# Random-feature attention and a feed-forward layer on one core: the weights' sign by a parametric ReLU, a fused sum and maximum for the keys, wider query instructions, float16 sums over the keys from unit 8 on

## The chip, the cores and the metric

The kernel runs on one core of a Trainium2 chip. The metric is the device time of one execution in microseconds, as the median of several runs; a run with the hardware profiler gives the trace. Engines are named as the profile names them: PE (TensorE, matmuls), PEld (its weight loads), DVE (VectorE), ACT (ScalarE), POOL (GpSimd), SP (SyncE, which issues the DMAs).

## The reference, cut to what matters

```python
# q, k, v: (8 batches, 8 heads, 576 tokens, 64); omega: (128, 64)
q_s, k_s = q * D ** -0.25, k * D ** -0.25
def phi(x):                               # 128 positive features
    h = x @ omega.T - (x * x).sum(-1, keepdims=True) / 2
    return np.exp(h - h.max(-1, keepdims=True)) / np.sqrt(128)
q_p, k_p = phi(q_s), phi(k_s)
kv = einsum('bhsm,bhsd->bhmd', k_p, v)    # sum over the keys
z  = k_p.sum(2)
attn = einsum('bhsm,bhmd->bhsd', q_p, kv) / (einsum('bhsm,bhm->bhs', q_p, z)[..., None] + 1e-6)
x = attn, heads side by side              # (4608 tokens, 512)
out = gelu(x @ w_in) @ w_out              # 512 -> 2048 -> 512; the weights come as float64
```

The term with the squares is the same for all features of a token and drops out with the maximum. So per pair of heads the kernel needs the projection by omega, a maximum per token, the exponential, the sum over the keys of exp(k) times (v, 1), and its product with exp(q).

## The kernel before, in words

**Attention** goes by units: one batch and two heads, 32 units of 2 x 576 tokens, four per batch. Units 0 to 7 are plain: float32 matmuls throughout. Units 8 to 31 are split: an operand becomes a high part and the rest, so that PE runs a quicker format. In a split unit `x_high` (L743, ACT) and `x_low` (L748, POOL) make the parts of q and k; `proj` (L756) projects the keys, two tiles of 128 tokens at a time into one PSUM tile, the product with omega's high part beside that with its rest; `proj_lo` (L760, ACT) copies the second half to SBUF; `proj_add` adds both halves (L769, DVE) and takes the negated maximum over the 128 features (L770, DVE). `k_shift` (L774, POOL) adds it. The queries are projected with the features on the partitions (`proj_q`, L778), turned in blocks by DVE (`q_blocks`, L781 and L783), their maxima combined and added (`q_shift`, L804). One `exps` (L555, ACT) then exponentiates keys and queries of the unit. `q_back` (L807, DVE) turns the queries back in four quarters of 288 columns, `q_high` (L810, ACT) rounds them, `q_low` (L813, DVE) takes the rest.

The sum over the keys has two forms. `kv` (L562) is a float32 matmul per tile; units 0 to 11 use it, each with its own v load (L512). Units 12 to 31 use `kv_split` (L853): exp(k) goes scaled into a float16 part (`k_high`, POOL's L307) and its rest (`k_low`, L842), v into a float16 pair by a scale of its batch (`v_a` L831, `v_b` L834; the scale comes from `v_max`, L877, and a chain of small steps), and two float16 matmuls per tile do the sum. v comes for a whole batch in one load (L524) into SBUF that block 0's weights held before. `num` (L619) multiplies by exp(q), `den` (L630, L624 for plain units) and `rcp` (L635 to L637) take the reciprocal, `div` (L667, L670) writes x.

**The feed-forward layer** goes by blocks of tokens: 256, 256, ten of 384 and 256. Block 0 is computed in float32 (`mm1` L1017, `mm2` L1043). Later blocks use float16 pairs, three matmuls per product (L1022; L1046 to L1048), with `gelu` (L1030), `g_high` (L1034) and `g_low` (L1038) between. Block 0 needs x of units 0 to 3 alone.

**The weights** come as float64, in 16 pieces (eight of w_in, eight of w_out) through two raw buffers (loads L373). Per piece `w_hi` (L377, ACT) scales the high words, read as float32, by 2^-112, which moves the exponent's bias; `w_lo` (L380, ACT) scales the low words; `w_shift` (L383, DVE) shifts the high words left by 3, which drops the sign; `w_sign` (L386, DVE) takes the sign bit of the raw word back in; `w_round` (L389, POOL) adds the low words' share; `w_max` (L392, DVE) takes the largest magnitude, from which the scales of the float16 pairs come (L419 and on).

**What sets the order.** No instruction is written at its place. A planner (`Planner`) holds all steps with a cost per step and a due time, and emits per engine the ready step that is due first; rings of buffers hold steps back. Due times come from `STARTS` (per block), `UDUE` (per half unit) and `OFF` (per step), and from bonuses in `X`. An engine then takes its instructions in exactly this order; so what waits holds what stands behind it.

## Time and profile before

| | |
|---|---|
| median of 3 runs | 990.48 us (990.17 to 991.42) |
| the profiled execution | 989.08 us, its span 986.9 us |
| granted PE clock, mean | 0.99 |
| busy: PE, DVE, ACT, POOL | 965.6, 759.7, 722.1, 338.5 us |
| moved by DMA | 70.91 MB |

In the rows below "x" is a count. A row of a stage gives each engine's busy time in the stretch, then the clock that was granted to PE. A row of a group gives the line, engine and operation, the tiles, the count, then after the bar the busy time in us and the mean ns of one, then the idle time of the engine just before them and who ended it. Float32 matmuls are two PE instructions each in the trace (a sum over the keys of one unit, nine matmuls, is x18). Matmuls overlap in the pipe, so their mean is longer than what one adds.

### The profile page before, as it was taken

The page shows a single profiled execution, that of the slowest core. Times are in us where ns is not written, and L with a number is a line of the kernel's source. Part 1 is how long each engine was busy: PE and PEld are TensorE (multiplying, and loading weights), DVE is VectorE, ACT ScalarE, POOL GpSimd, SP SyncE. Part 2 cuts the span into 40 slices and gives each one's busy share as a digit, 9 for nine tenths or more (in the row PEclk, how much of TensorE's full clock was granted, in tenths as well). Part 3 has the DMA queues.
Part 4 walks back from the last instruction along what each step waited for, and adds up shares of the span by engine and source line. Part 5 has one row for each costly group of instructions (what it writes and reads, how often), then busy time and mean ns, then how long its engine had stood idle before and what let it go on. Part 6 is the DMA issues. An engine that isn't in the chain of part 4 may idle for free.

```text
span 986.9 us, 17389 instructions
## 1 busy us (share of the span) xinstructions
PE 965.6 (98%) x5996; PEld 607.4 (62%) x5996; DVE 759.7 (77%) x1824; ACT 722.1 (73%) x1538; POOL 338.5 (34%) x528
## 2 busy tenths in 40 slices
PE   7789999999999999999999999999999999999998
PEld 6566676666666665666655666566656665555576
DVE  6988968988998989999988889888888897421111
ACT  6957849777888888888888877878778777442233
POOL 2334411345256435534443543544235431100000
PEclk8979999999999999999999999999999999999999
DMA  9854403432122131122312131112013100000000
GB/s 263 261 167 152 142 15 98 140 99 71 48 70 60 49 102 58 48 57 73 102 36 70 49 111 49 49 48 82 25 38 90 26 2 33 1 22 12 1 33 22
DMA packets 50647, 70.91 MB, mean 72 GB/s; under 512 B 18560, under 2 KB 27136, under 8 KB 50560
## 3 DMA queue, kind: packets, MB, share of 16 engines
q1 hardware_dynamic: 50560, 69.81, 23.8%
q8 instruction: 48, 0.79, 0.3%
q14 instruction: 39, 0.32, 0.1%
HBM read 60.36 MB, written 9.44 MB: 71 GB/s over the span
## 4 chain that ended last, share of the span: by engine, by line
PE 83%; DVE 8%; ACT 5%; DMA 2%; issue 1%; POOL 0%; SPq 0%; ACTq 0%; DVEq 0%
PE h L1022 32%; PE acc L1046 10%; PE acc L1048 10%; PE acc L1047 10%; PE at L619 3%; PE h L1017 3%; PE acc L1043 2%; PE at L778 2%; PE at L756 2%; PE at L853 2%; PE at L562 2%; PE at L531 1%; DVE gl L1038 1%; DMA raw<-in_w_in 1%; DVE nm L770 1%
## 5 line engine op out<-in xcount | busy, mean ns | idle before, releaser
L1022 PE MATMUL h<-xh,wih 128*128 128x384 f16 (+1 forms) x768 | 243.9, 318 | 1.2 <-DVE gl L1038 1.0
L1022 PE MATMUL h<-xh,wil 128*128 128x384 f16 (+1 forms) x768 | 243.7, 317 | 0.0
L1022 PE MATMUL h<-xl,wih 128*128 128x384 f16 (+1 forms) x768 | 243.7, 317 | 0.0
L748 POOL TENSOR_TENSOR r<-xt,r 64x256 fp32r<-64x256 f32 (+2 forms) x216 | 163.4, 775 | 187.7 <-ACT r L743 144.5
L1038 DVE SCALAR_TENSOR_TENSOR gl<-h,bs,gh 128x384 f16<-128x384 f32 (+1 forms) x192 | 113.1, 590 | 132.6 <-ACT gh L1034 131.1
L1046 PE MATMUL acc<-woh,gh 128*128 128x512 f16 (+1 forms) x544 | 205.3, 377 | 0.0
L1048 PE MATMUL acc<-wol,gh 128*128 128x512 f16 (+1 forms) x544 | 204.5, 376 | 0.0
L1047 PE MATMUL acc<-woh,gl 128*128 128x512 f16 (+1 forms) x544 | 204.5, 376 | 0.0
L1022 PEld LDWEIGHTS <-wih 128*128 128x128 f16 x1536 | 147.4, 98 | 83.0 <-issue 1.1
L1030 ACT ACTIVATE h<-h,bs 128x384 f32<-128x384 f32 (+1 forms) x192 | 102.7, 536 | 89.8 <-PE h L1022 85.8
L1034 ACT ACTIVATE gh<-h,bs 128x384 f16<-128x384 f32 (+1 forms) x192 | 107.7, 561 | 68.8 <-PE acc L1048 56.2
L1022 PEld LDWEIGHTS <-wil 128*128 128x128 f16 x768 | 75.1, 98 | 45.7 <-issue 4.0
L1048 PEld LDWEIGHTS <-gh 128*128 128x128 f16 x560 | 54.8, 98 | 62.6
L743 ACT CAST r<-xt 128x256 fp32r<-128x256 f32 (+2 forms) x216 | 81.4, 408 | 13.8 <-PE at L778 7.3
L1046 PEld LDWEIGHTS <-gh 128*128 128x128 f16 x560 | 54.6, 97 | 51.5 <-issue 1.1
L1047 PEld LDWEIGHTS <-gl 128*128 128x128 f16 x560 | 54.9, 98 | 46.1 <-issue 0.3
L670 DVE TENSOR_TENSOR w<-at,rt 64x128 f32<-64x128 f32 (+6 forms) x168 | 54.5, 325 | 3.4
L389 POOL TENSOR_TENSOR w<-w 128x1024 int32<-128x1024 int32 x12 | 29.7, 2474 | 66.0 <-DVE w L386 32.9
L756 PE MATMUL at<-om,r 128*128 128x256 f32 x216 | 50.6, 329 | 0.0
L778 PE MATMUL at<-r,om 128*128 128x288 f32 x192 | 49.3, 350 | 0.0
L813 DVE TENSOR_TENSOR ql<-qt,qh 128x288 fp32r<-128x288 f32 x96 | 43.9, 475 | 1.8 <-ACT qh L810 1.2
L630 ACT ACTIVATE dt<-at,vsc 64x288 f32<-64x288 f32 x80 | 39.7, 496 | 5.7 <-PE at L619 3.9
(223 smaller groups left out, 1773.6 us busy)
## 6 DMA issues: line engine op xcount, KB each, us to landing
xt<-in_kT SPq DMA_DIRECT2D x56, 288.0 KB, 4.0
xt<-in_qT SPq DMA_DIRECT2D x56, 288.0 KB, 3.7
out_x<-o SPq DMA_DIRECT2D x35, 256.0 KB, 2.0
raw<-in_w_in SPq DMA_DIRECT2D x16, 512.0 KB, 6.2
raw<-in_w_out SPq DMA_DIRECT2D x16, 512.0 KB, 4.4
w<-in_v SPq DMA_DIRECT2D x5, 1280.0 KB, 7.6
vt<-in_v SPq DMA_DIRECT2D x12, 320.0 KB, 3.8
out_x<-o SPq DMA_DIRECT2D x2, 128.0 KB, 1.9
```

The source lines that it names most:

```text
L670: nc.vector.tensor_tensor(x[r, c0:c1], ps[r, r0:r1], rt[r, r0:r1], op=ALU.mult)
L743: nc.scalar.copy(G['r', u, i][:, 0:b - a], xf[:, a:b])
L748: nc.gpsimd.tensor_tensor(r, xf[D:, a:b], r, op=ALU.subtract)
L756: nc.tensor.matmul(o[:, t], r[:, t * P:(t + 1) * P], om, start=True, stop=True)
L778: nc.tensor.matmul(G['pp', u, NK + g][:, 0:HS], om[:, i], G['r', u, NK + g], start=(i == 0), stop=(i == 1))
L1022: nc.tensor.matmul(h[:, 0:t], w, (G['xh', n, j], G['xh', n, j], G['xl', n, j])[k][:, 0:t], start=(i == 0), stop=(i == 3 * NJ - 1))
L1030: nc.scalar.activation(h, h, AF.Gelu, scale=G['bs', n][:, 2:3])
L1034: nc.scalar.activation(G['gh', n, c][:, 0:t], G['h', n, c][:, 0:t], AF.Copy, scale=G['bs', n][:, 3:4])
L1038: nc.vector.scalar_tensor_tensor(G['gl', n, c][:, 0:t], G['h', n, c][:, 0:t], G['bs', n][:, 3:4], G['gh', n, c][:, 0:t], op0=ALU.mult, op1 ...
L1046: nc.tensor.matmul(acc, gh[:, s], woh[:, c, c0:c1], start=(c == 0), stop=False)
L1047: nc.tensor.matmul(acc, gl[:, s], woh[:, c, c0:c1], start=False, stop=False)
L1048: nc.tensor.matmul(acc, gh[:, s], wol[:, c, c0:c1], start=False, stop=(c == NF - 1))
```

## The change

Line numbers of the changed kernel are a little higher; the steps keep their names.

- **Sign.** `w_hi` becomes a parametric ReLU with the same scale and a slope of 2^32 for negative words. That adds 32 to the exponent field of negative words alone, and `w_shift` moves just that bit into the sign's place. `w_sign` is gone, and `w_shift` is the last reader of the raw high words.
- **Maximum.** For pieces 2 and 3 of w_in, `w_abs` on ACT takes the sum of magnitudes (an upper bound of the largest) in place of `w_max` on DVE.
- **Sum and maximum of the keys.** `proj_add` is one fused instruction per tile of 128, with the maximum not negated; `k_shift` subtracts it. 216 tiles, and each is built as two instructions, one of 128x128 and one that writes 128x1; before there were 120 sums and 120 maxima, most of two tiles.
- **Queries.** `q_back`, `q_high` and `q_low` take two quarters at once: 576 columns, 48 of each instead of 96. The rings of `ql` tiles go from four of 288 to two of 576.
- **Float16 sums** from unit 8 instead of unit 12. Four v loads of a unit go, one of a batch comes.
- **Numbers of the planner**: all of `STARTS`, `UDUE`, `OFF`, some of `X` and some costs; `unit_split` is written in three parts with the same steps. So the order changes everywhere.

```diff
-X = dict(fb=94.6, fbp=-752.88, fb0=364.35, fbb=95.45, fbw=0.0, pm=0.144, tsw=1.28, wmaxp=0, plain=8, kvp=12, eb0=8, ttr=0)
+X = dict(fb=1419.17, fbp=-418.17, fb0=70.16, fbb=27.19, fbw=0.0, pm=0.15, tsw=1.28, wmaxp=0, plain=8, kvp=8, eb0=8, ttr=1,
+         pair=0, amax=12, qm=1, xm=0, km=0, prelu=1)
-STARTS = (352.72, 544.34, 271.08, 310.17, 157.51, 294.13, 523.44, 1198.62, 642.88, 445.45, 511.92, 981.52, 1405.68, 529.37)
+STARTS = (207.4, 1014.76, 655.98, -86.82, 177.65, 324.46, 422.08, 1469.57, 896.45, 1238.21, 1606.05, 2531.59, 2425.69, 1171.74)
...
     def w_hi(pc):
         hf = raw(pc)[2].bitcast(F32)
-        nc.scalar.activation(hf, hf, AF.Copy, scale=2.0 ** -112)
+        if X['prelu']:
+            nc.scalar.activation(hf, hf, AF.Prelu, scale=2.0 ** -112, alpha=2.0 ** 32)
+        else:
+            nc.scalar.activation(hf, hf, AF.Copy, scale=2.0 ** -112)
...
+    def w_abs(pc):
+        s = pc.l if pc.l is not None else raw(pc)[1]
+        nc.scalar.activation(s.bitcast(F32), pc.w, AF.Abs, accum_out=wmax[:, pc.win, pc.i:pc.i + 1])
...
-        op('DVE', 1.21, w_sign, pc, r=[rk, rk + ('hi',)], w=bk)
+        if not X['prelu']:
+            op('DVE', 1.21, w_sign, pc, r=[rk, rk + ('hi',)], w=bk)
...
-        if not X['wmaxp'] >> win & 1:
+        if X['amax'] >> (i + 8 * (1 - win)) & 1:
+            op('ACT', 1.3, w_abs, pc, r=bk, w=[('wmax', win, i)] + (pc.lk if pc.l is not None else [rk, rk + ('lo',)]))
+        elif not X['wmaxp'] >> win & 1:
             op('DVE', 1.21, w_max, pc, r=bk, w=[('wmax', win, i)])
...
+    def qv(t, g):
+        v = t.rearrange("p (a h s) -> p a h s", a=2, h=2)
+        return v[:, :, g] if X['qm'] else v[:, g // 2:g // 2 + 1, g % 2]
+
     def q_back(u, g):
-        nc.vector.transpose(G['qt', u, g], u.ef[:, slice(*XG[NK + g])])
+        nc.vector.transpose(G['qt', u, g], qv(u.ef[:, R2:], g))
     def q_high(u, g):
-        nc.scalar.copy(G['qh', u][:, g * HS:(g + 1) * HS], G['qt', u, g])
+        nc.scalar.copy(qv(G['qh', u], g), G['qt', u, g])
     def q_low(u, g):
-        nc.vector.tensor_tensor(G['ql', u, g], G['qt', u, g], G['qh', u][:, g * HS:(g + 1) * HS], op=ALU.subtract)
+        nc.vector.tensor_tensor(G['ql', u, g], G['qt', u, g], qv(G['qh', u], g), op=ALU.subtract)
...
-        for x, g in enumerate((0, 2, 1, 3)):
+        for x, g in enumerate((0, 1) if X['qm'] else (0, 2, 1, 3)):
```

The branch of `proj_add` that `ttr=1` now takes stood in the program before:

```python
for t in range(t0, t1):
    nc.vector.tensor_tensor_reduce(u.et[:, t], pp_k(u, i)[:, t - t0, 0], G['lo', u, i][:, t - t0], 1.0, -3e38, ALU.add, ALU.max, G['nm', u][:, t:t + 1])
```

Three places of the new order. The first is SP's queue at the very start; om is omega, xt are q and k of a unit, raw the weights. Before:

```order
1 L516 DMA xt<-in_kT 128x576
2 L516 DMA xt<-in_qT 128x576
3 L516 DMA xt<-in_kT 128x576
4 L516 DMA xt<-in_qT 128x576
5 L336 DMA om_66<-in_omT 64x128 x2
6 L373 DMA raw<-in_w_in 128x4x256 x4
```

And after:

```order
1 L338 DMA om_66<-in_omT 64x128 x2
2 L528 DMA xt<-in_kT 128x576
3 L528 DMA xt<-in_qT 128x576
4 L528 DMA xt<-in_kT 128x576
5 L528 DMA xt<-in_qT 128x576
6 L375 DMA raw<-in_w_in 128x4x256 x4
```

Omega's two loads moved from the fifth place to the first.

The second is DVE where x of unit 3 (xa) is written for block 0, and the last queries of unit 4 are shifted (et<-at,nm); rt and rc belong to the reciprocal, w_71 are the weights, wmax their maxima. Before:

```order
95 L386 SCALAR_TENSOR_TENSOR w_71<-raw,w_71 128x1024
96 L635 STREAM_TRANSPOSE rt<-dt 128x288
97 L636 RECIPROCAL rc<-rt 128x9
98 L637 STREAM_TRANSPOSE rt<-rc 128x288
99 L543 TENSOR_REDUCE nm<-at 128x4
100 L667 TENSOR_TENSOR xa<-acc,rt 128x256
101 L667 TENSOR_TENSOR xa<-acc,rt 128x32
102 L543 TENSOR_REDUCE nm<-at 128x4
103 L552 TENSOR_TENSOR et<-at,nm 128x512 x2
```

And after:

```order
87 L555 TENSOR_REDUCE nm<-at 128x4 x2
88 L648 STREAM_TRANSPOSE rt<-dt 128x288
89 L649 RECIPROCAL rc<-rt 128x9
90 L650 STREAM_TRANSPOSE rt<-rc 128x288
91 L564 TENSOR_TENSOR et<-at,nm 128x512
92 L680 TENSOR_TENSOR xa<-h,rt 128x256
93 L680 TENSOR_TENSOR xa<-h,rt 128x32
94 L564 TENSOR_TENSOR et<-at,nm 128x512
95 L397 TENSOR_REDUCE wmax<-w_71 128x1
```

The sign step ahead of it is gone, as six more above it are; one of the two last shifts moved ahead of xa. Above the place stand three maxima of weights now (L397), and five before (L392); two have become ACT's.

The third is PE at the sum over the keys of unit 8, between matmuls of the feed-forward layer (acc). Before, with vt the unit's v and et its exponentials:

```order
720 L1047 MATMUL acc<-woh,gl 128x512
721 L1048 LDWEIGHTS gh
722 L1048 MATMUL acc<-wol,gh 128x512
723 L562 MATMUL at<-vt_73,et 128x65 x8
724 L562 MATMUL at<-vt_73,et 128x130
725 L1046 LDWEIGHTS gh
726 L1046 MATMUL acc<-woh,gh 128x512
```

And after, with vb the float16 pair of v and w_71 the float16 exponentials:

```order
842 L1084 MATMUL acc<-wol,gh 128x512
843 L880 LDWEIGHTS w_71
844 L880 MATMUL at<-vb,w_71 128x129
845 L880 LDWEIGHTS w_71
846 L880 MATMUL at<-vb,w_71 128x65
847 L880 LDWEIGHTS w_71
848 L880 MATMUL at<-vb,w_71 128x65
849 L880 LDWEIGHTS w_71
850 L880 MATMUL at<-vb,w_71 128x129
851 L1082 LDWEIGHTS gh
852 L1082 MATMUL acc<-woh,gh 128x512
```

The sum is no longer one piece: its 18 float16 matmuls stand in groups with feed-forward matmuls between them.

## The prediction

> **What bounds the kernel now.** I read the page's busy row first, then the stages, then what TensorE (PE) waited for.

> ```profile
> span 986.9 us, 17389 instructions
> PE 965.6 (98%) x5996; PEld 607.4 (62%) x5996; DVE 759.7 (77%) x1824; ACT 722.1 (73%) x1538; POOL 338.5 (34%) x528
> ```

> The stages, each row with the stretch in us, its length, then the busy time of PE, weight loads, DVE, ACT and POOL, then the granted clock, the DMA share and GB/s:

> ```profile
> 0.00:25.00 25.00, 18.85 (x162) 16.26 (x163) 16.00 (x33) 15.72 (x45) 5.58 (x9) 0.86 0.92 264
> 25.00:50.00 25.00, 19.34 (x173) 14.20 (x174) 23.52 (x53) 22.79 (x61) 7.40 (x5) 0.97 0.85 254
> 50.00:75.00 25.00, 20.55 (x114) 15.47 (x113) 21.46 (x49) 14.60 (x23) 8.77 (x5) 0.75 0.55 166
> 75.00:100.00 25.00, 25.00 (x129) 16.08 (x126) 21.59 (x34) 18.47 (x27) 9.02 (x13) 1.00 0.43 148
> 200.00:800.00 600.00, 599.09 (x3668) 367.76 (x3666) 530.41 (x1344) 489.82 (x1078) 269.20 (x436) 1.00 0.21 62
> 900.00:987.00 87.00, 83.14 (x554) 53.96 (x552) 13.91 (x26) 28.85 (x57) 0.00 (x0) 1.00 0.05 16
> ```

> There are two regimes. From 75 us on PE is full; what shortens DVE, ACT or POOL there is worth nothing until one of them becomes late, and only PE work counts. Before 75 us PE is idle for 6.15 + 5.66 + 4.45 = 16.3 us and part of the time at a lower clock, while DVE is nearly full from 25 to 75. That is the second place where time can come from. At the end PE idles 3.9 us behind its last matmul, which the change doesn't touch. What PE waited for in the start, with the total in us, the times and the longest:

> ```profile
> PE at L600 <- ACT et L555: 3.3, 1, 3.3
> PE at L531 <- DVE om L339: 2.5, 1, 2.5
> PE at L531 <- ACT w L547: 1.8, 1, 1.8
> PE h L1017 <- DVE xa L667: 1.1, 1, 1.1
> ```

> The chain of waits behind these goes through the weights' DVE steps (start, us):

> ```profile
> 40.37 1.23 DVE w L386
> 61.45 0.43 DVE xa L667 x2
> 63.00 0.69 DVE et L552
> 63.71 2.13 ACT et L555
> ```

> L386 is the sign step that the change drops, and it stood on the chain. L667 writes the last rows of x that the first FFN block needs.

> **The PE work: float16 sums from unit 8.** The float32 sum over the keys (L562) takes 2.01 us of the chain per unit, for units 8 to 11, in a stretch where PE is full. The float16 sum (L853) has 18 matmuls per unit, so x360 are 20 units. The second row below is the chain's shares by line, the third the group (busy, mean ns of one, idle before):

> ```profile
> 195.25 2.01 PE at L562 x18
> by line: PE h L1022 32.1%; PE acc L1046 10.3%; PE acc L1048 10.2%; PE acc L1047 10.2%; PE at L619 3.1%; PE h L1017 2.8%; PE acc L1043 2.5%; PE at L778 2.4%; PE at L756 2.2%; PE at L853 1.6%; PE at L562 1.6%; issue 1.2%; PE at L531 1.1%; DVE
> L853 PE MATMUL at<-vb,w 128*128 128x65 f16 (+1 forms) x360 | 34.1, 212 | 0.0
> ```

> 1.6% of 986.9 is 15.8 us, 0.79 us per unit; four units go from 8.0 to 3.2 us: **-4.9 us**, all on the path. The busy column would give 34.1 / 20 = 1.70 us per unit and a gain of only 4 x 0.31 = 1.2 us, but a busy span holds the drain of each matmul, which lies under the next one; I keep 1.2 as the poor end.

> **The start.** In the stretch that ends when block 0 may begin, the stage row, then in it the busy time of L386 and of the maximum L392 alone, then the group of the 1024-wide ACT pass:

> ```profile
> 10.00:62.00 52.00, 42.69 (x363) 32.32 (x360) 48.08 (x99) 43.60 (x112) 16.96 (x11) 0.89 0.82 239
> 10.00:62.00 52.00, 8.51 (x7) 0.89 0.82 239
> 10.00:62.00 52.00, 6.05 (x5) 0.89 0.82 239
> L377 ACT ACTIVATE raw<-raw 128x1024 f32<-128x1024 f32 x16 | 18.6, 1164 | 0.6 <-DMA raw<-in_w_in 0.5
> ```

> DVE loses seven sign steps (8.5 us) and, by the new order, two of the five maxima (2.4 us): 48.1 becomes 37.2. ACT gains the two passes that replace those maxima, at the L377 row's 1.16 us: 43.6 becomes 45.9, and the Prelu in place of the scaled copy keeps L377's size (same tile, same count of operands but one constant; between 0 and +0.1 us each). So ACT is the next limit, and the stage can shrink by at most 52 - 45.9 = 6.1 us. ACT idles 8.4 us in it today, mostly behind DVE; I leave it 2.1 and take **-4** (ends -1 and -6.1).

> The omega load now stands first on SyncE, ahead of four loads of q and k, instead of fifth. PE waited 2.5 us for L339 behind it; the first k load is issued two DMAs later:

> ```profile
> 2.60 1.20 SPq L336 DMA_DIRECT2D om<-in_omT x2
> 0.74 0.39 SPq L516 DMA_DIRECT2D xt<-in_kT  x1
> SPq L373 <- DVE w L386: 25.8, 7, 7.9
> ```

> So 1.2 us of the 2.5 are lost again: **-1.3** (ends 0 and -2.5). The last row is SyncE's queue: loads of the next weights waited 25.8 us, in 7 waits, for L386 to release a raw buffer. The buffers come free one step earlier now; with DMA at 0.82 of its time I give that no gain of its own. The 3.3 us for the exponentials of unit 4 (L555) hang on L552 in a DVE queue that is 11 us lighter; ACT's own work ahead of them stays. I take **-2** (0 to -3.3).

> Two stretches of the start ran at a lower granted clock:

> ```profile
> 47.50:57.50 10.00, 8.64 (x55) 5.93 (x57) 8.05 (x20) 5.79 (x14) 2.55 (x2) 0.66 0.58 171
> 65.00:72.50 7.50, 6.62 (x29) 6.50 (x30) 6.10 (x14) 6.45 (x12) 2.37 (x1) 0.55 0.45 148
> ```

> Their loss is 8.64 x 0.34 = 2.9 and 6.62 x 0.45 = 3.0 us. One follows a wait of 1.8 us, the other one of 3.3. Shorter waits may spare one; I take **-3** (0 to -5.9). [...]

> **What lies beside PE, at no price while PE is full.** The groups that price it:

> ```profile
> L769 DVE TENSOR_TENSOR et<-at,lo 128x256 f32<-128x256 f32 (+1 forms) x65 | 25.2, 388 | 2.2 <-ACT lo L760 2.0
> L770 DVE TENSOR_REDUCE nm<-et 128x2 f32<-128x256 f32 (+1 forms) x65 | 25.6, 394 | 2.2
> L864 DVE TENSOR_TENSOR kvz<-at,kvs 128x128 f32<-128x128 f32 x20 | 5.7, 283 | 2.9 <-ACT kvs L860 2.7
> L894 DVE TENSOR_REDUCE vexp<-cg 32x1 f32<-32x4 f32 x13 | 1.8, 136 | 0.7 <-ACT cg L890 0.7
> L807 DVE STREAM_TRANSPOSE qt<-et 128x288 f32<-128x288 f32 x52 | 22.8, 460 | 3.6 <-ACT et L555 3.5
> L813 DVE TENSOR_TENSOR ql<-qt,qh 128x288 fp32r<-128x288 f32 x96 | 43.9, 475 | 1.8 <-ACT qh L810 1.2
> L884 DVE STREAM_TRANSPOSE ct<-cm 128x32 f32<-128x32 f32 x13 | 2.7, 205 | 0.0
> L842 DVE SCALAR_TENSOR_TENSOR w<-w 128x256 f16<-128x256 f32 (+1 forms) x50 | 21.2, 462 | 0.0
> L834 DVE SCALAR_TENSOR_TENSOR vb<-w,vsc,vb 128x640 f16<-128x640 f32 x20 | 17.9, 897 | 2.8 <-ACT vb L831 2.5
> L877 DVE TENSOR_REDUCE vmax<-w 128x1 f32<-128x640 f32 x20 | 15.8, 807 | 0.3 <-DMA w<-in_v 0.3
> ```

> The fused sum and maximum is one 128-wide instruction and one that writes 128x1, per tile. No row shows it. The nearest are L864 (two inputs, one in PSUM, 128 wide) and L894 (one column): 283 + 136 = 0.42 us. Before, a pair of tiles took 388 + 394, 0.39 us a tile. I take no change; the ends are 0.28 (the second part hidden) and 0.55 (two cycles per element by the slope below), -24 to +35 us of DVE over 216 tiles. The wider query instructions: (460 - 205) / 256 = 1.0 ns per column, so 576 columns cost 0.76 us and two of them replace four, for the transpose and the subtraction: 4 x (460 + 475) - 2 x (760 + 775) = 0.67 us per unit, 16 us over 24 units. Units 8 to 11 add L834, L877, five of L842, L864 and a 256-wide subtraction, about 4.5 us of DVE each, less about 0.5: +16 us. So DVE in 200 to 800 stays near 530 of 600 and PE covers all of it; if that cover went, each us of DVE over 600 would be a us of time. The one tight place is units 8 to 11, between 130 and 280 us, where the 16 us fall together and the wide instructions give back only 2.7; I put **+2** (0 to +6) there.

> **Sum.** The profiled execution is 989.08 us, its span 986.9 and 2.2 around it. -4.9 - 4 - 1.3 - 2 - 3 + 2 = -13.2, so 975.9. The median of the runs before, 990.48, is 1.4 above the profiled one: forecast **977.3**. All good ends give -22.7 (967.8), all poor ends +3.8, but they would have to come together.

> **Rivals.**
> *The start stays as long.* Loads and ACT set it, not DVE: DMA is at 0.82 there and ACT at 43.6 of 52, before two passes are added. Against it stand the waits for L386 and L667. Then only -4.9 and -1.3 remain: 984.
> *The start collapses.* All of it goes to ACT's floor and the clock stays up: -4.9 - 6.1 - 2.5 - 3.3 - 5.9 = -22.7: 968.
> *PE waits at the new sums, and the kernel is slower.* For units 8 to 11 the sum now needs v's maximum, its scales, both halves of v (L831, L834) and the split exponentials (POOL's L307, L842). PE takes its queue in order, so the FFN matmuls queued behind L853 wait too, and the load of v for two units' batches stands in SyncE's queue ahead of later q and k. The steps a unit gains are about 4.5 us of DVE. If PE waits more than 13.2 / 4 = 3.3 us per unit, the gain is gone; at 5 us and 20 in all it is 997. Against it: for units 12 on, PE idled 0.0 us ahead of L853.
> *The fused instruction isn't what it says.* DVE has 69.6 us idle in 200 to 800; it becomes the bound only from 0.39 + 69.6 / 216 = 0.71 us a tile on, well above the range.

> **How the numbers follow.** Forecast 0.68, the long start 0.15, the short one 0.08, PE waiting at the new sums 0.07, the slow fused instruction 0.02. The range runs from 967 (the short start) to 987 (the long start with the gain of the sums halved, and a us for the tight place) and leaves out little more than the slower cases. What a measurement here can tell from no change is about 0.2%, 2 us. Faster: 0.68 + 0.08 + most of the long start, 0.87; within 0.2%: the long start's poor end, 0.05; slower 0.08.

> **What would show it.** PE full from about 65 us instead of 75, with less than 9 us idle before; DVE under 40 us and ACT near 46 in the stretch up to block 0; the sums of units 8 to 11 at about 0.8 us of the chain each; fused tiles near 0.42 us; PE still over 99% in 200 to 800. It is wrong if PE shows waits at L853's successor in 180 to 280 us, if DVE passes 95% after 200 us, or if PE's idle time before 75 us stays near 16 us.

## The result, and the profile after

The changed kernel takes 980.18 us (median of 4 runs, 979.91 to 980.60), the kernel before 990.33 on the same chip (4 runs, 988.29 to 991.42). The ratio is 0.9901, with a 95% interval of 0.9889 to 0.9913: 10 us faster, where 13.2 were worked out.

The profiled execution took 980.60 us with a span of 978.4. The busy row of the page:

```profile
span 978.4 us, 17554 instructions
PE 960.2 (98%) x5996; PEld 598.8 (61%) x5996; DVE 716.2 (73%) x1935; ACT 729.0 (75%) x1507; POOL 355.8 (36%) x552
```

TensorE (PE) issues as many matmuls as before and is busy 5.4 us less; the span fell by 8.5, so 3.1 us come from its idle time. VectorE (DVE) lost 43.5 us of work. The stages, with the columns of before (stretch, length, busy PE, weight loads, DVE, ACT, POOL, granted clock, DMA share, GB/s):

```profile
0.00:25.00 25.00, 17.90 (x135) 14.66 (x137) 10.17 (x28) 14.37 (x38) 5.60 (x9) 0.80 0.89 251
25.00:50.00 25.00, 23.98 (x231) 18.10 (x227) 21.58 (x56) 23.86 (x67) 7.78 (x5) 1.00 0.82 252
50.00:75.00 25.00, 21.91 (x138) 16.47 (x137) 20.37 (x51) 19.50 (x31) 10.47 (x10) 0.93 0.61 179
200.00:800.00 600.00, 597.83 (x3692) 363.58 (x3691) 513.56 (x1455) 498.51 (x1042) 272.52 (x441) 1.00 0.21 59
```

PE's idle time before 75 us is 7.10 + 1.02 + 3.09 = 11.2 us, where it was 16.3. Between 200 and 800 us it is 2.2 us, where it was 0.9. The stretch up to block 0, and below it the longest rows of what PE waited for in the whole run (total us, times, longest):

```profile
10.00:62.00 52.00, 43.24 (x353) 33.43 (x354) 39.39 (x95) 46.01 (x114) 17.42 (x11) 0.90 0.85 246
```

```profile
PE at L613 <- ACT et L559: 3.7, 1, 3.7
PE h L1058 <- DVE gl L1074: 1.5, 4, 0.6
PE at L543 <- DMA xt<-in_kT: 1.3, 1, 1.3
PE at L575 <- ACT et L568: 1.3, 1, 1.3
```

DVE in that stretch went from 48.1 to 39.4 us and ACT from 43.6 to 46.0. The wait for unit 4's exponentials (L568, before L555) fell from 3.3 to 1.3 us. The wait of 2.5 us for omega is gone: PE starts its first projections at 5.26 us instead of 7.73, and then waits 1.3 us for the second load of k. New is the first row: unit 0's transposes (L613) wait 3.7 us for its exponentials. With that wait the lead is gone, for the sum over unit 0's keys starts at 16.84 us, where it started at 16.03 before. Later PE gains again: the seventh matmul of block 0, the first that needs the last rows of x, starts at 57.22 us instead of 61.84.

### The profile page after: what moved, and what is told of

The parts are those of the page before. It is cut to its first block, busy times and chain, and to the rows that moved or that the text cites. A ratio compares the mean times of both kernels' runs of the same rounds, so it can differ in the third digit from the quotient of the medians.

```text
span 978.4 us, 17554 instructions
## 1 busy us (share of the span) xinstructions
PE 960.2 (98%) x5996; PEld 598.8 (61%) x5996; DVE 716.2 (73%) x1935; ACT 729.0 (75%) x1507; POOL 355.8 (36%) x552
## 4 chain that ended last, share of the span: by engine, by line
PE 86%; DVE 5%; ACT 4%; DMA 1%; issue 1%; POOL 1%; SPq 1%; ACTq 0%; DVEq 0%; POOLq 0%
PE h L1058 33%; PE acc L1082 11%; PE acc L1084 10%; PE acc L1083 10%; PE at L632 4%; PE acc L1079 3%; PE h L1053 3%; PE at L801 2%; PE at L779 2%; PE at L880 2%; PE at L575 1%; PE at L543 1%; DMA vt<-in_v 1%; PE at L623 1%; POOL r L771 1%
## 5 line engine op out<-in xcount | busy, mean ns | idle before, releaser
L771 POOL TENSOR_TENSOR r<-xt,r 64x256 fp32r<-64x256 f32 (+2 forms) x216 | 177.0, 837 | 188.9 <-ACT r L766 107.1
L1058 PE MATMUL h<-xh,wih 128*128 128x384 f16 (+1 forms) x768 | 243.8, 317 | 1.7 <-DVE gl L1074 1.5
L1058 PE MATMUL h<-xl,wih 128*128 128x384 f16 (+1 forms) x768 | 243.8, 318 | 0.0
L1058 PE MATMUL h<-xh,wil 128*128 128x384 f16 (+1 forms) x768 | 243.7, 317 | 0.0
L1074 DVE SCALAR_TENSOR_TENSOR gl<-h,bs,gh 128x384 f16<-128x384 f32 (+1 forms) x192 | 112.7, 588 | 140.0 <-ACT gh L1070 137.7
L1058 PEld LDWEIGHTS <-wih 128*128 128x128 f16 x1536 | 146.6, 98 | 84.0 <-issue 0.9
L1058 PEld LDWEIGHTS <-wil 128*128 128x128 f16 x768 | 75.1, 98 | 47.1 <-issue 4.1
L779 PE MATMUL at<-om,r 128*128 128x256 f32 x216 | 55.2, 341 | 0.7 <-POOL r L771 0.7
L643 ACT ACTIVATE dt<-at,vsc 64x288 f32<-64x288 f32 x96 | 47.6, 496 | 8.6 <-PE at L632 4.6
L648 DVE STREAM_TRANSPOSE rt<-dt 128x288 f32<-128x288 f32 x64 | 30.3, 473 | 17.0 <-ACT dt L643 12.0
```

What stands on the lines that cost most here:

```text
L771: nc.gpsimd.tensor_tensor(r, xf[D:, a:b], r, op=ALU.subtract)
L779: nc.tensor.matmul(o[:, t], r[:, t * P:(t + 1) * P], om, start=True, stop=True)
L1058: nc.tensor.matmul(h[:, 0:t], w, (G['xh', n, j], G['xh', n, j], G['xl', n, j])[k][:, 0:t], start=(i == 0), stop=(i == 3 * NJ - 1))
L1074: nc.vector.scalar_tensor_tensor(G['gl', n, c][:, 0:t], G['h', n, c][:, 0:t], G['bs', n][:, 3:4], G['gh', n, c][:, 0:t], op0=ALU.mult, op1 ...
```

## Four parts, one at a time

Each of the four kernels that follow is the changed one with one part undone. In the first three the order of all other instructions on every engine is exactly that of the changed kernel; the fourth changes a number that the planner reads, and is planned anew with the changed kernel's tables. The kernel before, run beside them, has 989.73 us (21 runs). The changed kernel's 980.18 us come from other runs, in which the kernel before took 0.6 us more than here, so the differences to it below are good to about half a microsecond. A fifth part, the two maxima moved to ACT, was not undone alone.

**The sign step put back.** Behind each of the 16 shifts the old step runs again; on weights whose sign the Prelu has already set it changes nothing.

```
     def w_shift(pc):
         nc.vector.tensor_scalar(pc.b, raw(pc)[2], 3, None, op0=ALU.logical_shift_left)
+        nc.vector.scalar_tensor_tensor(pc.b, raw(pc)[2], -2 ** 31, pc.b, op0=ALU.bitwise_and, op1=ALU.bitwise_or)
```

> The changed kernel with the old sign step put back right behind each of the 16 shifts, at the same place of an otherwise unchanged order (16 more DVE instructions of 1.2 us; it writes the bits that stand there already). Theory (the start is DVE's, and the sign step held it): DVE rises by 8.5 us in 10 to 62 us, to about 48, and the 12th matmul of block 0 comes 4 to 7 us later than at 62.9 us; the whole is 984 to 987. Rival (ACT, at 46 of 52 us there, already sets the start, and the gain came from the new order): under 1.5 us, 980 to 982.

Measured: 990.2 us (11 runs, 989.09 to 990.99), ratio to before 1.0008 (0.9999 to 1.0017). This one step, 16 instructions of 1.2 us, is worth 10.0 us in the new order, as much as the whole change. The time is 3 us above the range of the theory, the nearer of the two. DVE's work from 10 to 62 us rose by 4.5 us alone, to 43.9, since less of the other work fell into that stretch. Where the 10 us arise is asked further down.

**The fused sum and maximum taken apart again.**

```
-        if X['ttr']:
+        if 0:
...
-        nc.gpsimd.tensor_tensor(es, es, ..., op=ALU.subtract if X['ttr'] else ALU.add)
+        nc.gpsimd.tensor_tensor(es, es, ..., op=ALU.add)
```

> The changed kernel with the fused sum and maximum of the keys taken apart again into a sum and a negated maximum of two tiles each, at the same place of an otherwise unchanged order (240 DVE instructions for 432). Theory (DVE lies beside PE from 75 us on): within 1 us of 980.2, whatever DVE's busy time does. Rival (the fused form freed DVE and PE followed): 2 to 6 us more. The trace gives the price of both forms, 0.42 us a tile for either by my estimate.

Measured: 987.19 us (11 runs), ratio 0.9976 (0.9967 to 0.9985), 7.0 us over the changed kernel and a microsecond above the rival's range; the theory fell. Its stage from 200 to 800 us, and its largest wait in the whole run:

```profile
200.00:800.00 600.00, 593.52 (x3662) 360.69 (x3661) 538.81 (x1276) 493.28 (x1033) 271.01 (x440) 1.00 0.21 60
```

```profile
PE h L1058 <- DVE gl L1074: 7.5, 13, 1.1
```

DVE has 25.2 us more to do there, though it still idles 61 us; PE loses 4.3 us of busy time. The loss comes in small waits: the first FFN matmuls of a block's next part (L1058) wait for `g_low` (L1074), 13 times with 1.1 us at most, where the changed kernel has 1.5 us in 4 times. In all 13 cases DVE was at work up to 0.03 us ahead of `g_low`, so it is DVE's queue that was late, and not what `g_low` reads.

**The query instructions narrow again**, each of the three (transpose, copy, subtraction) as two of 288 columns:

```
-        nc.vector.transpose(G['qt', u, g], qv(u.ef[:, R2:], g))
+        for h in range(2):
+            nc.vector.transpose(G['qt', u, g][:, h], qv(u.ef[:, R2:], g)[:, h])
```

> The changed kernel with each of the wider query instructions issued as two of 288 columns, at the same place of an otherwise unchanged order (48 more transposes, 48 more casts on ACT, 48 more subtractions). Theory: DVE and ACT each rise by about 10 to 16 us, PE stays full, within 1 us of 980.2. Rival (DVE or ACT is late somewhere in 200 to 800 us, and the width paid): 2 to 6 us more.

Measured: 984.13 us (5 runs), ratio 0.9945 (0.9932 to 0.9957), 3.9 us over the changed kernel, within the rival's range. The same wait has grown, with DVE only 7.0 us busier in 200 to 800 and 10.3 in all (line numbers are 3 higher here):

```profile
200.00:800.00 600.00, 596.17 (x3673) 361.82 (x3670) 520.54 (x1537) 498.53 (x1082) 270.82 (x441) 1.00 0.21 59
```

```profile
PE h L1061 <- DVE gl L1077: 2.4, 6, 0.7
```

That is 0.9 us more than in the changed kernel; the rest of the 3.9 us lies in no single row.

**The float32 sums back for units 8 to 11**, `kvp=8` to `kvp=12`.

> The changed kernel with units 8 to 11 back at float32 sums over the keys; the planner orders it anew from the same tables. Theory (each float32 sum costs PE 1.2 us more in a stretch where PE is full): PE busy 4 to 6 us more, 984 to 986. Rival (the new DVE and POOL work of these units cost the start's gain again): 978 to 981, with less PE idle time in 150 to 300 us.

Measured: 983.23 us (5 runs), ratio 0.9939 (0.9926 to 0.9951): the part is worth 3.0 us, a little under the theory's range. Its busy row:

```profile
PE 965.6 (98%) x5996; PEld 604.6 (62%) x5996; DVE 704.4 (72%) x1902; ACT 721.4 (73%) x1494; POOL 343.3 (35%) x528
```

PE has 5.4 us more busy time than in the changed kernel, but its idle time is 981.5 - 965.6 = 15.9 us instead of 18.2, with DVE 11.8 us lighter. So the float16 sums give back some of their gain in waits, as far as two orders that were planned apart can be compared.

The four parts together come to 10.0 + 7.0 + 3.9 + 3.0 = 23.9 us, more than twice what the change brought. The parts can't simply be added, and the next runs ask why.

## Steps against order

Besides the steps, the change brings new tables (start times, due times and offsets), from which the planner sets the order. Two kernels cross the two, and a third makes one part alone with the tables of before. The kernel before, run beside them, has 990.1 us (9 runs).

**Old steps, new tables:** the changed kernel with

```
-X = dict(..., kvp=8, eb0=8, ttr=1, pair=0, amax=12, qm=1, xm=0, km=0, prelu=1)
+X = dict(..., kvp=12, eb0=8, ttr=0, pair=0, amax=0, qm=0, xm=0, km=0, prelu=0)
```

> All steps as before (sign step on VectorE, separate sum and maximum, 288-column query instructions, float32 sums up to unit 11), but planned with the changed kernel's tables, so that the omega load comes first and the due times are the new ones. Theory A (the gain is made by the steps, and the new order is only fitted to them): undone one at a time in the new order, the four steps cost 10.0, 7.0, 3.9 and 3.0 us, 23.9 together, though the whole change is worth 10; with all undone the planner may move things around, so I expect 990 to 1000, slower than before or equal to it. Theory B (part of the gain is the order's own): 983 to 988, faster than before.

Measured: 1021.84 us (5 runs), ratio 1.0324 (1.0303 to 1.0345).

**New steps, old tables:** the changed kernel with `STARTS`, `UDUE`, `OFF` and the first five numbers and `pm` of `X` from before.

> All steps as in the changed kernel, but planned with the tables of before (omega load in fifth place again). Theory A (the steps make the gain, but in an order made for other work they bring less): 982 to 988. Theory B (steps alone do it, the order is immaterial): within 2 us of 980.2. If it came out at 990 or above, the order would carry the whole gain.

Measured: 1013.09 us (5 runs), ratio 1.0234 (1.0211 to 1.0258).

**The float16 sums alone**, the kernel before with `kvp=12` to `kvp=8`, and its own tables:

> The kernel before with one part alone, the float16 sums from unit 8, planned with the tables of before. The prediction's term is -4.9 us on the path, 1.2 at the poor end; undone from the changed kernel it measured 3.0. Theory A (PE's work sets the time there): 990.3 less 3 to 5, so 985 to 987.5. Rival (the old VectorE queue, longer by 16 us for the new splitting and without the wide instructions, delays the FFN matmuls as it did with the parts undone): 989 to 991, no gain.

Measured: 1016.99 us (4 runs), ratio 1.0272 (1.0246 to 1.0298).

None of the theories held: all three are 23 to 32 us slower than before, far outside every range given. The second one had a further reading on record, that at 990 or above the order would carry the whole gain. It doesn't, since the new tables with the old steps are slower still. In the first two kernels a few steps have no offset in the other's table (`w_sign` in the new, `w_abs` in the old) and go without; the third keeps its own table, and shows the same. The waits of the last one, its longest rows:

```profile
PE h L1022 <- DVE gl L1038: 7.8, 13, 2.0
PE at L756 <- POOL r L748: 3.4, 2, 2.6
PE at L600 <- ACT et L555: 3.3, 1, 3.3
PE at L562 <- DMA vt<-in_v: 2.7, 1, 2.7
```

and two of its stretches, a stage in which PE was full before and a piece of it at half clock:

```profile
200.00:400.00 200.00, 189.03 (x1143) 116.06 (x1141) 183.44 (x454) 160.53 (x351) 93.20 (x151) 0.96 0.24 72
281.60:295.20 13.60, 8.91 (x34) 6.02 (x34) 12.16 (x39) 9.65 (x34) 9.69 (x21) 0.50 0.30 86
```

No engine is full here: PE is busy 189 and DVE 183 of 200 us. PE waits in many places, a few us each, for DVE, POOL, ACT and a load, and part of the stage runs at half clock on top (the 13.6 us of the second row; the stage's mean clock is 0.96). The rival named for this run, the longer DVE queue ahead of `g_low`, is in the first row (1.0 us in the trace before), but with 7.8 of the 24.8 us by which the two spans differ it is only a part.

So the tables are fitted to the durations of one set of steps. With other steps the same tables give an order that costs 23 to 32 us, two to three times what the change is worth. The change is steps and refitted tables together, and no run here prices the one without the other. It also fits the sum of 23.9: undoing a part measures the part plus the misfit of an order that was made with it, and with all steps undone the kernel is 41.7 us above the changed one. How the 23.9 divide into the two was not measured. That the order is fitted so closely is shown; that a fit of the old steps to a new order would find nothing better than 990 was not tried.

## Where the sign step costs its 10 us

The sign step was put back behind half of the shifts: in one kernel behind the 8 that start by 64 us, in the other (`> 8` in the diff) behind the 8 that start at 70 us or later. The unaltered changed kernel ran on the same chip, and the kernel before has 989.21 us there (9 runs).

```
+    shifts = []
     def w_shift(pc):
         nc.vector.tensor_scalar(pc.b, raw(pc)[2], 3, None, op0=ALU.logical_shift_left)
+        shifts.append(pc)
+        if len(shifts) <= 8:
+            nc.vector.scalar_tensor_tensor(pc.b, raw(pc)[2], -2 ** 31, pc.b, op0=ALU.bitwise_and, op1=ALU.bitwise_or)
```

> The changed kernel with the sign step of before put back behind the first 8 of the 16 shifts (those that start at 13 to 64 us), the order otherwise the same. All 16 cost 10.0 us, and in that trace 4.0 us were lost by 55 us and the rest from 62 to 128 us. Theory A (the prediction's: the price lies in the stage up to block 0, where VectorE is nearly full): 8 to 10 us, so 988 to 990. Theory B (half of it is the later pieces' own): 4 to 5 us, 984 to 985.

Measured: 983.93 us (5 runs, 983.34 to 984.32), ratio 0.9942 (0.9929 to 0.9954).

> The same with the sign step behind the last 8 shifts alone (those that start at 70 to 121 us), where TensorE (PE) has no wait of over a microsecond in the changed kernel. Theory A (what lies beside a full PE has no price): 0 to 1 us, so 980 to 981. Theory B (the weights of the second matrix are late for block 1, whatever came ahead): 4 to 6 us, 984 to 986. If both halves came to much less than 10 together, they hide behind one another.

Measured: 985.29 us (5 runs, 984.91 to 985.56), ratio 0.9955 (0.9943 to 0.9968).

> The changed kernel unaltered, on the same chip as the three other runs of this call, so that a few us can be compared: 979.5 to 981 by its earlier runs, half clock at 14.6 to 24.8 us and once more near 62 us.

Measured: 980.28 us (4 runs, 979.28 to 980.35), ratio 0.9903 (0.9889 to 0.9916), as expected.

The halves cost 3.7 and 5.0 us, 8.7 of the 10.0: they add up nearly, and more than half lies behind 62 us, where the prediction had put nothing. Theory B holds for the second half; the first is just under B's range and far from A's. The stretch from 62 to 130 us in the changed kernel, then in the kernel with the late signs, and the longest rows of what PE waited for in the latter from 62 to 140 us:

```profile
62.00:130.00 68.00, 68.00 (x375) 45.57 (x374) 57.46 (x112) 51.92 (x83) 28.28 (x25) 0.97 0.46 148
```

```profile
62.00:130.00 68.00, 64.34 (x358) 42.59 (x358) 63.18 (x107) 50.64 (x79) 25.52 (x22) 1.00 0.46 148
```

```profile
PE at L618 <- DVE et L569: 1.8, 1, 1.8
PE at L436 <- DVE vb L1164: 1.0, 1, 1.0
PE at L548 <- DVE kvz L589: 0.6, 1, 0.6
PE at L442 <- DVE ct L439: 0.4, 1, 0.4
```

PE has no idle time at all there in the changed kernel, and DVE has 10.5 us to spare. With eight steps of 1.2 us more DVE is left 4.8 us, though some of its other work has slid behind 130 us, and PE idles 3.7 us, half of it for a unit's shifted tiles (L569, line 564 of the changed kernel). Another 1.0 us follows at 132.7 us, at the transpose of the weights' maxima (L436), which comes after DVE's last work on the weights; in the changed kernel PE idles nowhere from 62 to 140 us. A full PE doesn't show how little slack the engine beside it has.

## The clock in the start

In the changed kernel's first 75 us two stretches run at half clock. The rows for the window ahead of the first one, the stretch itself, and the same for the second one:

```profile
11.20:14.60 3.40, 0.00 (x0) 0.00 (x0) 1.84 (x3) 2.83 (x6) 0.16 (x1) 0.99 1.17 318
14.60:24.80 10.20, 9.11 (x47) 7.92 (x49) 3.32 (x8) 7.77 (x24) 4.74 (x3) 0.50 1.01 263
...
58.90:62.30 3.40, 2.23 (x20) 2.23 (x21) 2.83 (x11) 3.37 (x5) 2.35 (x1) 1.00 0.41 107
62.30:65.70 3.40, 3.40 (x15) 2.92 (x14) 2.73 (x8) 3.35 (x9) 1.16 (x1) 0.51 1.18 317
```

The first follows the 3.7 us wait of L613. **The first wait filled:** matmuls of zeros, whose result the transposes overwrite, stand ahead of unit 0's transposes.

```
     def q_trans(u, g):
+        if u is units[0] and g == 0:
+            for i in range(34):
+                nc.tensor.matmul(G['pt', u, g][:, 0:256], z16[:, 0:P], z16, start=True, stop=True)
```

> The changed kernel with 34 more matmuls of zeros ahead of unit 0's transposes, in the 3.7 us in which TensorE (PE) waits for the first exponentials; their result is overwritten, and the order is otherwise the same. In the changed kernel the granted clock is 0.5 from 14.6 to 24.8 us, right behind that wait. Theory A (the wait is what halves the clock, and PE's lost time at half clock, at most 5 us, is on the path): the clock stays at 1 and the time falls by 2 to 5 us, to 975 to 978. Theory B (the clock falls with the wait, but ScalarE and the weights set the start, 46 of 52 us): the clock stays at 1, the start is shorter at 25 us, and the end moves by less than 1 us. Theory C (the low clock has another cause): half clock stays, and the time is the same or slower by up to 1 us.

Measured: 978.15 us (4 runs: 975.52, 978.02, 978.27, 978.72), ratio to before 0.9877 (0.9855 to 0.9898). The same two stretches in the profiled execution, the one of 975.52:

```profile
11.20:14.60 3.40, 3.40 (x35) 3.01 (x32) 2.08 (x4) 3.40 (x8) 0.42 (x1) 1.00 1.19 318
14.60:24.80 10.20, 9.39 (x86) 7.96 (x86) 6.02 (x13) 10.20 (x32) 4.49 (x3) 1.00 1.09 282
```

PE does 81 of the program's matmuls (and five of zeros) instead of 47 in the same 10.2 us, and ACT, which stood behind it, is busy all the time. In this execution theory A holds: with the wait filled the clock stays at 1.00 in both rows, and the time is 4.7 us under the changed kernel's 980.18, so the half clock was on the path. It is the one execution of the four with no half clock at all (mean clock 1.0). The other three have a mean clock of 0.996 or 0.997 (the changed kernel 0.992 to 0.995), so about half of the half-clock time was left there, and by the medians 2 of the 5 us were won.

**A second wait filled as well:** six matmuls on the identity ahead of unit 4's sums.

```
     def kv(u):
+        if u is units[4]:
+            for i in range(6):
+                nc.tensor.matmul(G['pk', u][:, 0:P], ident, ident, start=True, stop=True)
```

> As the kernel with the filled first wait, with six more matmuls of 128 columns (on the identity, result overwritten) ahead of the key sums of unit 4, in the 1.3 us for its exponentials at 59 to 60 us. Of the executions with the first wait filled, one had no half clock at all and took 975.5 us, the others a mean clock of 0.996 to 0.997 and 978.0 to 978.7. Theory A (the wait at 59 us, 0.9 and 1.3 us within 3.4, brings the second stretch of half clock): no half clock in any execution, 974.5 to 976.5, so faster than both kernels. Theory B (the second stretch has another cause): 977.5 to 979, as with one wait filled.

Measured: 978.46 us (4 runs, 977.34 to 979.35), ratio 0.9883 (0.9867 to 0.9899); clock 0.997 and 0.998. Theory A's time fell, and B's came true, though not for B's reason. The trace shows where the rest is:

```profile
15.40:18.90 3.50, 2.18 (x15) 1.76 (x15) 1.30 (x2) 3.50 (x9) 2.16 (x1) 0.99 0.91 215
18.90:25.70 6.80, 6.80 (x39) 5.21 (x37) 3.06 (x8) 5.23 (x19) 2.55 (x2) 0.50 0.99 289
```

Behind the filled wait PE waits for the first v, 1.2 us in this execution, and the next 6.8 us run at a clock of 0.50; in the one without half clock the wait was 0.8 us, and the clock stayed at 1.00. The second stretch, near 62 us, is gone, as A had it.

Both filled kernels are faster than before. Against the changed kernel they are 2 us faster by their medians; on the same chip the runs of the second one touch its runs at one end (979.35 against 979.28), so the gain is likely but small.

## Why the prediction came out, point by point

The forecast was 977.3, and 980.2 came. The direction and the two stages were right; the price of DVE's work beside a full PE was wrong, the gain of the sums was too large by a fifth, and a loss of 2.2 us spread over unchanged steps wasn't in the sum at all.

**The start, -10.3 in all (-4, -1.3, -2, -3).** In the traces PE's idle time before 75 us fell from 16.26 to 11.21 us, by 5.05; the prediction had named less than 9 as its sign. For the clock the stretches at half clock of before, the first two of which the prediction had left out, are:

```profile
7.70:11.10 3.40, 3.37 (x32) 3.37 (x32) 1.78 (x4) 0.53 (x3) 0.00 (x0) 0.50 1.00 303
17.90:21.30 3.40, 3.40 (x23) 2.90 (x22) 3.40 (x8) 3.40 (x15) 0.10 (x1) 0.50 0.94 299
48.60:55.40 6.80, 6.54 (x35) 4.64 (x37) 5.48 (x11) 4.08 (x8) 2.35 (x1) 0.50 0.63 189
65.70:72.50 6.80, 6.62 (x29) 6.50 (x30) 5.40 (x13) 5.75 (x12) 2.37 (x1) 0.50 0.50 163
```

In the changed kernel the sum over one unit's keys took 4.19 us at 16.84 us, at a clock of 0.50, and 2.28 at 25.51, at 1.00: 1.84 times as long. By the clock of 0.50 I count half of PE's busy time there as lost, an estimate (by the 1.84 it would be 46%): (3.37 + 3.40 + 6.54 + 6.62) / 2 = 10.0 us before, (9.11 + 3.40) / 2 = 6.3 after, 3.7 less, where 3 were forecast. The start gained 5.05 + 3.7 = 8.8 us instead of 10.3. Within it the exponentials of unit 4 gave the 2.0 of the text. Omega's wait of 2.5 us became one of 1.3 for k, the 1.2 that was worked out, but the next wait took it back. The 3.7 of the clock are partly luck: the two late stretches, which the text argued from, lost 6.6 us before and 1.7 after, 4.9 less, while a new wait of 3.7 us made a stretch of 10.2 us at 14.6, which the sum didn't have, and the early loss rose from 3.4 to 4.6. ACT's 46.0 us in the stage up to block 0, where 45.9 were worked out, are luck too: the stretch now holds the exponentials of unit 4 (2.12 us) and a table load (1.28) that came later before, and one pass over low words and four exponentials less. DVE came to 39.4 instead of 37.2, with four maxima in the stretch and not three.

**The sums, -4.9.** The chain of waits of the changed kernel has "PE at L880" with 2.2% of 978.4 us, 21.5 us for 24 units, 0.90 us each instead of 0.79:

```profile
by line: PE h L1058 32.8%; PE acc L1082 10.5%; PE acc L1084 10.4%; PE acc L1083 10.4%; PE at L632 3.5%; PE acc L1079 2.9%; PE h L1053 2.8%; PE at L801 2.3%; PE at L779 2.2%; PE at L880 2.2%; PE at L575 1.3%; PE at L543 1.1%; DMA vt<-in_v 1.
```

The 0.79 were too low for the kernel before as well. If PE's busy time is divided among its instructions, each counted from the end of the one ahead of it and half clock counted half, the float16 sums took 17.9 us for 20 units before and 21.6 for 24 after, 0.90 us each in both, and the float32 sums 24.7 and 17.0. So the new sums save 7.6 - 3.7 = 3.9 us of PE's work, not 4.9; in the kernel before the chain runs through only 15.8 of the 17.9 us, so its share was too small a measure. Undone, the part was worth 3.0. The rival of PE waiting at the new sums didn't come: PE waited 0.2 us in all for L861 ahead of L880.

**"What lies beside PE, at no price while PE is full": this step failed**, in its price and in its rule. The price first. The fused instruction by the names that the trace has for it, the sum in two rows and the read of the maximum in a third; then the time in which DVE was busy with any of the three, over the whole span:

```profile
L789 DVE CUSTOM_DVE_ANT_0 et<-at,lo 128x128 f32<-128x128 f32 x117 | 28.5, 284 | 5.0 <-ACT lo L783 4.7
...
L789 DVE CUSTOM_DVE_ANT_0 w<-at,lo 128x128 f32<-128x128 f32 x99 | 23.8, 282 | 1.1 <-ACT lo L783 1.0
...
L789 DVE DVE_READ_ACCUMULATOR2_ANT nm<- 128x1 f32 x216 | 17.6, 82 | 0.0
```

```profile
0.00:978.40 978.40, 53.15 (x432) 0.99 0.25 72
```

The three rows make 69.9 us, but they overlap: in the trace the read of one tile (282.653 to 282.736 us) lies under the sum of the next (282.653 to 282.938). So it is 53.15 us for 216 tiles, 0.25 us a tile, below the good end of 0.28 and far from 0.42. The same view of the kernel before, for the sums (L769) and for the maxima (L770):

```profile
0.00:986.90 986.90, 46.24 (x120) 0.99 0.24 72
```

```profile
0.00:986.90 986.90, 47.23 (x120) 0.99 0.24 72
```

That is 93.5 us for the same 216 tiles, 0.43 us each; the text took half of a mean that contains single tiles, 0.39. So the fusion takes 40 us from these lines, and not nothing; taken apart again, DVE's whole busy time was 34.7 us longer (750.9 against 716.2). The wide instructions were sized better one by one:

```profile
L840 DVE TENSOR_TENSOR ql<-qt,qh 128x576 fp32r<-128x576 f32 x48 | 38.4, 807 | 2.8 <-ACT qh L837 2.7
...
L834 DVE STREAM_TRANSPOSE qt<-et 128x576 f32<-128x576 f32 x26 | 19.6, 765 | 10.6 <-ACT et L568 10.6
```

765 and 807 ns, where 760 and 775 were worked out. But the narrow ones overlapped too (before, 96 subtractions of 475 ns, 45.6 us in all, kept DVE busy for 43.9), and putting them back cost DVE 10.3 us and not 16. Then the rule: in a fixed order, 25 us more of DVE work cost 7.0 us, 7 us more cost 3.9, and eight late sign steps 5.0, all beside a PE that the rows of the changed kernel show as 99.6 to 100% full. In the other direction the rule does describe what happened: PE was full in 200 to 800 us before and couldn't gain from a lighter DVE there, and it didn't; its idle time even rose from 0.9 to 2.2 us.

**What was given back, +2.** Idle time rose by 1.3 us in 200 to 800 and 0.7 elsewhere behind 75 us, in all the 2.0 of the forecast, which had put them on units 8 to 11 alone. Start and sums make -8.8 - 3.9 = -12.7, the idle time +2.0, and the span fell by 8.5: 2.2 us more are busy time of PE. The same division of its busy time puts them on steps that didn't change, the projections of the queries (+1.1), those of the plain units (+0.8) and those of the keys (+0.6) above all, which now stand beside other matmuls; why they cost more there was not tested. The sum misses the profiled pair by 4.7 us (-8.5 for -13.2), the medians by 2.9: the profiled execution of before lay 1.4 us under its median, that of the changed kernel lies 0.4 above.

## What to carry to other kernels

Where an order is fitted to durations, no part has a price of its own: cost a part with the order refitted, and read a part undone in the fixed order as an upper bound, since a refit could keep that order. The idle time of the bound engine (0.9 of 600 us here) limits what can be gained beside it, and says nothing on what a longer step there will cost; for that, look at the slack of the queue that feeds it, stage by stage. Price a step by the time in which its engine is busy with all of its lines, not by adding the means of records that overlap. After a change of the start, look for the first long wait on TensorE and for the clock behind it (here 3.7 us, and 0.50 for the next 10.2), and fill the wait if it can't be removed (2 us here, by the medians).

## What the hardware did that was not expected

The profiles of the kernel before and of the changed one, cut on their grids of 3.41 us, have 549 such windows at full clock ahead of 960 us, 274 and 275. Of the 537 in which TensorE idled less than 1.0 us none was followed by half clock; of the 9 with 1.0 to 1.6 us 3 were (1.53 us at 14.5 and 1.58 at 45.2 before, 1.14 at 58.9 after); of the 3 with more, 2.50 and 3.17 before and 3.41 after, all 3. So in these two traces the idle time within a window goes with the clock of the next one, and from 1.0 to 1.6 us both clocks follow: 1.37 us at 4.3 us of the changed kernel was followed by full clock. In the kernel with one wait filled 1.32 us of idling were followed by full clock too:

```profile
52.20:55.60 3.40, 2.08 (x9) 1.17 (x7) 3.40 (x8) 1.93 (x2) 0.00 (x0) 1.00 0.67 224
55.60:59.00 3.40, 2.58 (x23) 2.58 (x24) 2.83 (x9) 3.37 (x5) 2.35 (x1) 1.00 0.56 153
```

In that with two, the 1.32 us from 15.4 to 18.9 us (above) were followed by half clock. What decides there was not tested; the same kernel does have executions with and without a stretch (mean clock 1.0 and 0.996 with the first wait filled). In the two traces the six stretches of half clock ahead of 960 us last one to three windows, and in all six the last window is one in which TensorE idles for 0.05 us or less (14.6 to 24.8 us above: 1.1 us idle in the first window, none in the other two).

The record that writes the maximum out took 82 ns for 128x1 on VectorE, and the one that writes the sum out on ScalarE 579 ns, behind a pass of 1435. Below these rows is the time in which ScalarE was busy with the two passes and their reads together, 3.05 us:

```profile
L401 ACT ACTIVATE w<-w 128x1024 f32<-128x1024 f32 x2 | 2.9, 1435 | 0.0
...
L401 ACT ACTIVATION_READ_ACCUMULATOR w<-w 128x1 f32 x2 | 1.2, 579 | 0.0
```

```profile
10.00:62.00 52.00, 3.05 (x4) 0.90 0.85 246
```

So a maximum moved to ScalarE costs 1.5 us there, since the read starts under the pass, and not the 1.16 of the forecast. (That pass sums magnitudes, which is a bound on the maximum.) The Prelu, with its slope for negative words, takes 1195 ns, where the scaled copy took 1164:

```profile
L380 ACT ACTIVATE raw<-raw 128x1024 f32<-128x1024 f32 x16 | 19.0, 1195 | 0.6 <-DMA raw<-in_w_in 0.6
```
